# A planner's margin in front of TensorE steps goes from 80 to 200, and its table of ranks is replaced

## The chip, the cores and the metric

The kernel runs on one core of a Trainium2 chip. The metric is the device time of one execution in microseconds (us). Before the change the median of three runs is 565.36 us (565.08 to 565.58). The engines are TensorE (PE in the profile, PEld for its weight loads), VectorE (DVE), ScalarE (ACT), GpSimd (POOL) and SyncE (SP, which here only issues DMAs).

## The reference

Two layers over 2048 tokens of width 640 in bf16, each an attention block and a feed-forward block on layer-normed input, both with a residual:

```python
x = A_x
x = x + _A_ref(_layernorm(x), A_wq, A_wk, A_wv, A_wo, A_beta)
x = x + _B_ref(_layernorm(x), B_w1, B_w2)
x = x + _A_ref(_layernorm(x), A_wq, A_wk, A_wv, A_wo, A_beta)
x = x + _B_ref(_layernorm(x), B_w1, B_w2)
```

`_B_ref` is relu(x w1) w2 with an inner width of 1728. `_A_ref` has 32 heads of width 20 and goes through four segments of 512 tokens one after the other. Within a segment it is causal softmax attention; beside it each head reads a memory matrix M (20 x 20) and a vector z that were summed over the earlier segments, and the two results are mixed by a gate per head:

```python
logits = einsum('bhqd,bhkd->bhqk', qs, ks) * scale + mask
p = softmax(logits); a_dot = einsum('bhqk,bhkd->bhqd', p, vs)
a_mem = (phi(qs) @ M) / (phi(qs) @ z + 1e-6)
o = g * a_mem + (1 - g) * a_dot
M = M + phi(ks)^T vs;  z = z + sum(phi(ks))
```

## The kernel before

**The work.** There are eight segment passes: layer 0, segments 0 to 3, and layer 1, segments 0 to 3. A pass consists of `ln1` (layer norm and its transposition), `proj_kq` (L951, the keys and queries), `proj_v` (L998), `relay` (the last twelve rows of each head group are moved to a second tile, `kqL`), `scores` (L1290), `apply` (L1372), `mem_write` (L1153), `mem_read` (L1240), `o_turn`, `out_proj` (L1536), `ln2` and `ffn` (L1590 for w1, L1602 for its rest, L1620 for w2). One pass has 20 rounds of scores, so 160 in all. A round needs two PSUM slots of two banks each, X and Y, both free: TensorE fills them with a few narrow matmuls, ScalarE takes the exponential of each (L1304 and, where two head groups share a round, L1301), GpSimd masks the diagonal blocks (L1280), and the next round can start. Three more PSUM banks, MISC, serve all other matmul groups; VectorE or ScalarE empties them.

**What sets the order.** Nothing in the engines' streams is ordered by hand. Each of the parts above is a Python generator, and the class `Sched` simulates all engines with fixed costs and picks one step after another. The order in which it picks them is the order of the instructions on each engine; on the chip each instruction then waits for its semaphores and for nothing else. So a number of the planner changes the chip's time only through the order. (And through filler: where TensorE's planned gap, less 150, leaves room for two or more 128-wide matmuls, `_filled` emits that many matmuls on the identity, L779.) For each candidate step `_best` computes the earliest start, L292:

```python
r = ready + SEM_NS + (PE_MARGIN if e == "pe" else 0.0)
```

`ready` is the planned end of the last of the results and slots that the step needs. The candidate with the earliest start wins; between steps of the same start, the one with the lower `due`. The costs are in `mm_ns`, `dve_ns`, `act_ns` and `xbar`; a change of TensorE's mode (full array, `row` for scores, `col` for apply, `half` for L1602) is planned at `MODE_NS` = 100. The planner also holds packed VectorE operations and GpSimd's operations apart (`port`), and the crossbar transposes have the constants `XB_NS`, `XB_TILE`, `XB_LAT` at L163.

**The dues.** `plan` is run twice. The first plan takes its dues from the paced streams (`paced`, `each`) and serves only to list the keys of all steps. The second takes `due` from `TABLE`: a packed list of differences, one for each step of the sorted keys, whose running sum is the rank of that step (`ranked`). There are 5082 steps, and the ranks are a permutation of 0 to 5081. So the table says which of several steps that could start at the same time goes first; it doesn't fix the order by itself.

**The loads.** SP and ACT fetch the first four token tiles, wv, wk and wq; POOL fetches the other tokens, wo, w1 and w2 later, each DMA waiting for the one before (`loads_pool`). w2 lies over the keys and values of the first pass and is fetched after that pass is done with them.

Of the kernel before, what the change touches and what calls it, by code (L numbers as in the profile page):

```python
# [13 lines left out]
T = 2048  # L14
D = 640
H = 32
DH = 20
NSEG = 4
L = T // NSEG
# [3 lines left out]
G = H // 4  # L23
# [134 lines left out]


SEM_NS = 60.0  # L160
PE_MARGIN = 80.0

XB_NS, XB_TILE, XB_LAT = 200.0, 27.0, 2300.0  # L163
MODE_NS = 100.0
# [25 lines left out]
class Sched:  # L190
# [89 lines left out]
    def _best(self, op, resv=None):  # L280
# [10 lines left out]
        for k, (e, hold, tail, make) in enumerate(op.alts):  # L291
            r = ready + SEM_NS + (PE_MARGIN if e == "pe" else 0.0)  # L292
            if e == "dve" and op.port:
# [118 lines left out]


TABLE = """
c-
n1R3$UbBaqjcK=AZZ6xpVK_yZ5p8?t595eYq@;1$JR!c?v{8kw79EETSf2qA4q(QWdQz<Y6UPL9HYtWYIEZV#TCVR5YmslLBKBtPm=ZQV~UwW!
b&UF6`cC=j-pB`DZR=P0i!~&pF+Fy8Cp0-T!QJd!-~dOIb4cp<XB>@?J?Lk+12nRPfp^Z^36-
UeV1`#rGSypWwAwuExCEu&N@lJfj!m>MChq&ZIo4TS4<CjBJ+U`m|nv8F$Jzbr<H$;q$a!Cv|B_j@29Sz67hLr6b?g2jri0w=8Q-
y0WNiG4>X$ZDBl?{h+x?YBCBc-`6qlIRpw05-;e449SI<)xc{}_d(8W5`jkp?<vgMi8~I|w&43byd&)6a?pD_=%w<a-
YW;>eC%pW{!^!LZx`m;tZ{HGLkBr%tIlI58P@wf@5WeL4uk$MMxV!?a`~b@g8Q%N>yRji>_(*|-  # L420
_aZJYa4#GF*66%A*{>6C&G9IGG2_|b<mvGtD%Qo_*KR1??UHJcF;Bs``U)PdnwC`e)Pm1?0>&p3)}6IJ#q#3z7y|jWvd*N3t*XD@(%3jR?N9w*
2x{<u@|zx8+*J5JNgjxcNlZu4SqMtFUsAxelK=(6=r=zHsJT2Shqp01OMyg98fwecj4FhptT?RJomLjkm?`d4J-
O#@GU_PpIba6PwS#ONc%^yV$R)NApfR&u+xavO0hTCES|uQGii!>nb~auBP~!F0-Xui@?p6K-
eVSN<CS5ojNb{ZKMD<g3u{wIa#&{Nlx~DnZS15C9!*fGgK7@X*o^n}@>y`mWG!|wfwk-KYYo2bl?U!s_}h9=eFA)HSib>&If>cl;{Gu1bwG6ss
LwzXyCB{Bu%d!>LzufBJhsYN?Sfhhv`yxVAc1+sTGB7!eN?w&b_aWJ;ob)B$ziXf@+$O{z`M4Bb4+hYq0<sprSzXBR*!)87&yHIeVaeV;O*oaJ
XtAb=J>YvR?N=jIo$$n*WfXm<PY^{aWBGq0-
qVR?_~X43!ia#C!Argm}lGJmkW0y`e<)%k3z)XahTVmYIkD!W4(_f{g;haIHR}LQ?GzmG{DVfrSO{!+K8~L1$t5$r=r49lWq~3Q8oRnsOc$|`!
O;aXg-4Lt4K?+W?5Cu!foo^d~Z6)>7_C*_FXRcyYShYWplEyM?b?X6^D5yOG3I);2HBXDQGpqu6x&c&{Pucoz-
%<7tvy8)a$}zPYe6l{2J({ytZ#IOLdh@#&uYZ@Ol|CoP)V5n(#WOm)N(BlsIBkY~?VmR)#F&xMO>ofd_T)t4wYs+<i@_@p}lXUWQG~PmjUh%`O
S7^gUhD1+^%Z1!=vNGg*T6-p~d(wm`pvxjp$!_X+)cNqas};eJdfQDKLzh@J_gTc$7kSSLZ%RxRsE9i_ZEuN_Z<l75AL5e-  # L430
<;_L+l|r(^Sa8tYrm>$gS!^EU9SM=&oVl^iF~@qCx%4<re8bcIi+)J%`_DQ&K@V5QKC_mCX2N8!B1!N1*4IVJPRhP^R=Z@WCJy%{c0&%!zF-
;bonB__w7kN0)!cd()^=pbTrj<|C0oJ0l9SjvUZxgc{c5fMWi&cEMHGT`}Hpq~|IBO)C?K8Ep9Sf@Hf8ed|@H$SO{`F3}S7BY=B3jJvCp8o!tg
`T2;y~e?UCV?_?BwSr8ex;1NZa{Wd_)tPVt%9m6?A3dh26R6-?gr+&fid?}#`>?A5g-
c@B_iJN6vwEE>VU5dA!FE_^##`w<9WjPGaGE?<QH%!#oT`MPKr3~BSv4oI`tHT&b&se_8P6yKvbLnhZxZc(R3bKtiLIu#;f$vw^_U@{zn6vU(K
m+MSGPBy9{dEBaCQO{&F}ijy|}g=0T+pzk6$H!DmxwHUctjQh%>$CFsG?w*I8X#U3L>vYc@wLd>osE=`3o$830!{CCJ=r!kt4hw3upltrr)>&+
TV;PVpXX@_{&+hr5fESj1R*cmX5zN(IK&D$=O*F#+JuQ{!T$Q47PO4#$VdXFw+2MMT@Lqy3aX&L-
2&m`eI$E0s7Kd*Oi{UXoCB4{r$V)~UaaLbR>#}uRKb-
m0TGzZRHFX!3!&H9y9v8Oh0x?B;3E3(L4dfIVe|DMg<svI4?=}sg*f~AGW`t@lMnG$+u6mo^n9xjYUj4yrKClQPMUCS_S=)Z><T#+*zqeuUq*Z
PWP%rk~UmzXclhPY>T8j%-t9ak@CDRA=|j=9p?U^zr3&+%)>u#F($Qa}b3*f|SX%V*k@+-3`HCBY_++1_i!<SK>J?xUx_TM2l|5qa3!Qt-
)T)LO^j+b3}~gIcMJ`bPDA@{qm)uQxg`0%tDj_jSFzUmjCK1Ygyo`g8J>-YI{AN=Ws;^dTV8am@NPxnJk>S^YhE0=%BXno-nFcgx51wEn654)p  # L440
9$jXc1!G_OAZDn8AeKc~+C<(Gqg%|8}_Tuy7x1I`AFIOxSOHE|9;pVu>*2mSTVX~ffaT7Aw_jf%{4R{iNXixc*GutOE=hOje_kUnzkI%ci&SQA
g<H0(hoWfemmuM%R3;r}-3vK!?mh$%DB(<~yjMVGhXuGMfgyjyr>j6FGC4ZNpfL;J(Hw-xg<R4YFtpL88mEL&KoSaoPs(#x)i&ni|9qgENF9N%
-7U_}Fz%iuQzYIS*jZk+M5MGTvSeMYO|jbk)3zvznh>2iSr1~Xa`GEtd1cqN>cQqa4N-b5sj(~s-H23GZ&MbZIO;sVmJc#?z@*o)gqxT-
LcdKpUL<YfbSBf*|`NK(Z9nE2DOcn`Uq2~pgmlRj>b0yekU)F}{7{Y|+eCGCILi+H`L`->QPexR5H{F8=V`Bm)!DqcI0^rM-tHWKD=7siqTcU9
sV>A3+U=vW0NMXi>HeC08$=Q35qIWM7~TMbcUN#hXXmvshynBmM>RJzBllQdxEtU&J>z0_9@GeK{0K<14%<>#N^Oqa;F#EwhPyZUiGE9~<)xb@
|agO$^OC@mwVq+~I<#5@qO7WTAi)ZGd!I#kqAQP8d{>d8Ki_>9|06crOMd+(~P!d$)%@fu#ztk{|P>j~{+WYa{o$O`jnCv`#lo^Kj{Y|f&Vga6
+y*UNj5|98u;%H3FJU6?E78o2_pd}1+|<9a!CavC(hO}&~7Ejg-
=vB_iU8hkUB@2aouO)Fh|e_bO+7xVG|!TV9IvWL=wm8_5QTWY<g68P)`x3YXpV|E~F>{w;IZc^XZ$Q_t>J$UUwgqy?;ty5z$wG&RR>C!ZQ5cmH
AQEd-&vRl0uR+-
T&j55oRp~}eBmA#PR@8Txr)@A!jj(Bwh(JPZ{xu2>$sYmn?%4eOiR4$FIpEV=LR?HF?GM?J~CUJH`>$Wj_2FUils3x00_eU$^lwpXS!;~GtRK|  # L450
&XwqWj7yw^u-*e5)`QbA;{GlotuI=rTvC1<y!0V)UZedMI-SxMbp(RI<T=x^M?`I5X<OYGS==<P6O{wDM`&f0VbyKld(W+Cen9T4k<K14g!Fyo
+1L@n?hlEctto0*_a6qYmg+BrWY&%lm*vCEsII{P&n)v9|tg)QvCDwI0>t4_a*aZ(Rq)y}8^FB+C}S)(16e^JxC_sdkOtS&cz+X2kq99884(Av
-Q<fQj$*0;{8X>AhoE&$ixkE|a$CY$t_?w~h$+vc=DgVr+L?Zn!nu!D8k?xnno0i*S5CVx&1>)wdb=YfA??m2}vy7Enp>6;nG_RAMEWkk0w=*#
-JTA!<f>sfi%tDjGH$DfKGjJ_NlaHH<+b0+l@#L8EY+djN6k_YLbb$W^AkTSGnC*@YguL@&JD^z@jpRaV5OU^ReWZ;|9+kc>+#_9ZPZ7`O1#Ln
MF#()no7L4%zFe~UG+T-cSu?t|`>l28jR;5`d?{}#IZ|4g8cH5XEu5s3dEb+{)5TQ-
7=lBWiswTfdAFndc)#zc5Qjc}Ug*IjPXa0+*FlO2NTrb~ZH1E<zlXJ`3aMpR5W$)q^%&E(zq3?7X`;&&r*MYuawOc@Ml4rOMpU#-
^NANw4S5tPfub2@fKTa)LCK!f)T#T!K)f>RGi`PE(+-t-iWxP!GF>oHn7$Q%!9U5!O<;cHwPOXc34(RS<*EM1XKMVb+Q8`~eDc3<aHQ27k4ps-
WW-z{oQqE$YsKx#D?qQ6XpWMe-K1J)ACT7^hZ$pv;pftiWXU`s{SuMYH?$cN`#QyP6h}jWOO&1#bAY-DTz8ujz3OTlh_XF_!wbWc5D(HyyvsGq
y(K^$Ng0I5^;?Uul*Si>BtP5S1R=}W5)?XGcCZRcdn$ZMh-
?y`Kx!+yMPI*R+?vxJEM$E|ZF`TCotJGG=f*zB#<yYjxw95)`a3+<2dM!qu0mmC5T^ZV}QI=XjDmhN^ZO~j595%AE?CS!H`6q#4FM}?-  # L460
JR|Rb7x~WcY3z6Qv~|J8*}I+x9zOx}`3CBO9Y6r*VdOQ}V)nfd9Bqe(To>_Z7}}e~^@#kfi`ZX32NG|FTpw^}^aa!p9|WgKNbwZrw;{_GBHFqv
VNQb@9D+V_`NCWe>C_999|aV#5^C~Z_thhxG$5F0pabXYKSM)LI_u0gafZ_Zw=HQ@pvg4ggpH{B##o=_MJ<>PbPp_w7(#df2;HzxuUFT@L6gu=
Z}u^G<|g)}Ew`+J{)Sk2WdYfgLs!FAA9A)LFQl%q$6X0N)8sts{?}xIUD`H%Bw-
!rv6`L0@qp1)A9HW+E=KSISM*);kZr~oZ)|ioeaR79_ABI`6>f3ys_srybXuc;-
~HX;FrE%n^EuIH6guTGW9&n2K}VsJobhL{S01nGrX57gjs|M<IN<31?z|M@;!yYYDu@MW`-
uL0$X53LOMNHT_7Py29pdefcAmI7DL8!&{@20v9L6mIO++R5Wm~@Ls&X$p`qvTX4<V!eue02Hz5JD{AgZmAkGr~j241|*jqzE}?Z;K8LG`Fscp
8tPu3rQC$JKY7U*+=(+q*rpxQ56s2gM^RXVk6gfczQWmqL=Yp}U$f|HZ(YksL=>wdnpf-mQuu&MKt5#bp8i<jhfLUCO9qr`0+YUuIviArHDNWd
0#o5b-~%Fj{w6!CoRib{T7kj1?w4d2UJ!Yo&YwXJ~Z-8oUry@j6zvP0Y#gYZ;N_GF1EfC~KARe-
<;x5Ft{mIjbFfE@D=f^1iOyKyOhk!k^MEJMZfef7f7^Jz=#~Q;>U1#wlH0UPLU|4ysqk57{;7Ad8&B%r3pIgn3(W?xw^#5!<2tG3H~~2lRH3(j
?>=2OnR@b%+(Z>`~8R&bUkyr>w=^c4Phq>}ee+Zv>Y$SUG~ZqZl3H{#uZzLrU9Vaf|zHXm>%+WhS3MoL<l8-  # L470
&3Hv0R9d3Ypok#v2PtUGs`~5PVk=Q6PYQZvT68n7b{2Tm4^{m%gp0lR(C7<9z^r)(C09pI5%;B98xVpzT=43Cv`1%UE;_xb~OtA)8uFLruc+o6
7LB_c(cb0pZFiwE;Z9)-
fs}~8iM)d6KQyoo%4BRLLY0h)~hk*#zdiI;`WTSMv2)yXWUY?NN?1ZwNB6M)$w)6WP7kKs(IQs)UbtR;1*9wg_yO*C*~zcWO292Y?%fWn38*qa
`c{pm04d^nI$q_Wqb;p^B)N@XVjS!az>Awb!bkcRw9*zTodsXTf%Nm9I#)R)kSabS$G~{{TTZnMVr*Cz_h#ZIl++%ck8RUD(0CVRYSMF%<nc)Z
jI5vSBH7vU*}ayjF|)!krNM%u=-DVWn*=sxoX%;ovVHAUg4A2JnW^!)fHl%l=VoN+R12Z-vb&Z+H7!kllVBJ?uMzCGx{!h3Yn)t4VzD-
)I$O<9^=kDl1alq8yb+cLaWz<<-DC*jA*qWX+jNm7^!ov%h(IBZdi=-
XY+>{x8guKV*RzOhVv|ko?=B*BaSH(|M^Ip@nqVJ4mFU`nk7E5s<3xvHfmApmEc8&WRC$uMXV*-
)P!|TeZAMFw|MQl;Q34N;Tm_jmpdu5KCA>ktTWztX>$HHtDGCKX&Nx4{g>oc*{5HD$3Msa2zV}L_i<9}NuRUAirG1h=~dpgWoo6u-
bhOQ=E3h1UT4e!Ilancw5Jt4&&h+A4D%`5I-
Y|@IN2@C?9dBiV9%#C3LaDqepHiQA2mb#>5}6p{NXgD+jAnJcK=yFirMc+q%kVvI2~2)>jR+Mkr(u8M4yA;enZs8%C(?p(Q!q;<Wff5wX7UU@+  # L480
`8jWv5?41~fkZ;nsl4QN0nfHiF`#ZZptn9XqfS*p&NE{zK@`=izymS<*j&|GHcjo|f3NjwUj6hx7g(IPMw!Z1I#S4qZIoIeSqbE>Kgy8{NlCd8
iod-%BoZ8hf~83wG)Tkmwk4%`l`r5dMo%VyAKma-7jxfyfrv-
}c>rh}A+Ix`rwLL*&Af(L6kliRI#`IUrR|^jP9QED~C5j`(!&Nu|eD{^XuwZ?yvi?O09B$V>VuS03nGYO(KR;OR(QV84uBw!%1JShG9ulsh4=U
C{^K6@^Y+(Ftx0;Juz~_i&$8<h;Yg)JgGd((_#oNdG1Izwm#6l+ngNuWN-4brk-
eWRY`>_;k2H#71Sh*h!!NpUZb(u^oK!wW&bDlSQ{XD{Q-_&_q%^N%ED6|G!f4ADojtpYiqC8hE?yDdy9PNd6y@&HNb
"""


def one(fn):
    return lambda *s: [(lambda e: fn(e, *s), True)]  # L490


def pe(ns, make, waits=(), acq=(), users=1, mode="full", hold=()):
    return Op([("pe", ns, 190.0, make)], waits, acq, users, mode, hold=hold)

# [1219 lines left out]
```

## Time and profile before

| | |
|---|---|
| median of three runs | 565.36 us |
| the profiled execution | 565.58 us, span 563.8 us (1.8 us outside the span) |
| TensorE matmul | 5115 instructions, 556.4 us busy (99%) |
| VectorE, ScalarE, GpSimd | 420.9, 422.5, 214.9 us busy |
| granted TensorE clock | 1.000 over the span |
| first matmul; first scores; first w1 matmul; last scores | 1.25; 19.07; 108.73; 472.96 us |

A busy matmul time of 99% says little by itself: each matmul is shown with its whole way through the array, so neighbours overlap. What a matmul costs is the distance from its start to the next one's start. Where the page says that an engine was idle before an instruction, it names what ended the idle time.

### The profile page before, as it was taken

What the parts mean: (1) busy time and instruction counts of PE and PEld (TensorE: products, weight loads), DVE (VectorE), ACT (ScalarE), POOL (GpSimd) and SP (SyncE); (2) the same over time, 40 slices, a digit from 0 to 9 for tenths busy, and PEclk for the clock granted to TensorE, in tenths of its full rate; (3) what the DMA queues carried; (4) which work ended last, traced back from release to release, by engine and by line L of the source; (5) the groups of instructions that cost most, each with busy time, mean ns of one, the idle gap of its engine ahead of it and who ended that gap; (6) DMA issues with size and microseconds to landing.
All of it is one profiled execution on the core that took longest, in us unless ns stands there. A gap on an engine that the chain in (4) does not pass through costs nothing.

```text
span 563.8 us, 12521 instructions
## 1 busy us (share of the span) xinstructions
PE 556.4 (99%) x5115; PEld 297.7 (53%) x5118; DVE 420.9 (75%) x1024; ACT 422.5 (75%) x517; POOL 214.9 (38%) x341
## 2 busy tenths in 40 slices
PE   8999999999999999999999999999999999999997
PEld 5454455445555445644546454565545654755655
DVE  6789989998998878857689956998778876424202
ACT  3899999999889878688897978878898778023140
POOL 3664546454454343452345433244333443002000
PEclk9999999999999999999999999999999999999999
DMA  6435787776534343573255451565116531431201
GB/s 221 129 90 133 152 145 150 226 153 106 90 70 85 57 72 62 81 119 76 44 82 106 80 84 20 96 124 93 33 19 91 99 82 20 86 73 36 59 1 47
DMA packets 126609, 50.62 MB, mean 90 GB/s; under 512 B 112120, under 2 KB 124600, under 8 KB 126552
## 3 DMA queue, kind: packets, MB, share of 16 engines
q1 hardware_dynamic: 124568, 42.19, 40.3%
q0 software_dynamic: 1552, 7.29, 4.5%
q8 instruction: 40, 0.66, 0.5%
q10 hardware_dynamic: 432, 0.34, 0.2%
q14 instruction: 17, 0.14, 0.1%
HBM read 15.16 MB, written 7.37 MB: 40 GB/s over the span
## 4 chain that ended last, share of the span: by engine, by line
PE 91%; DVE 5%; ACT 2%; DMA 1%; issue 0%; SPq 0%
PE ps L1590 21%; PE ps L1620 20%; PE ps L951 15%; PE ps L1290 9%; PE ps L998 8%; PE ps L1536 7%; PE ps L1372 7%; DMA wv_r<-in_A_wv_dram 1%; PE ps L1153 1%; PE ps L1240 1%; ACT PT L1304 1%; DVE x_sb L1478 1%; PE ps L1602 1%; DVE stats L868 1%; DVE stats L869 1%; PE ps L1096 1%
## 5 line engine op out<-in xcount | busy, mean ns | idle before, releaser
L1304 ACT ACTIVATE PT<-ps 128x1024 bf16<-128x1024 f32 x256 | 248.3, 1024 | 42.9 <-PE ps L1290 42.1
L1280 POOL TENSOR_SCALAR_AFFINE_SELECT PT<-PT 128x512 bf16<-128x512 bf16 x256 | 173.1, 692 | 235.8 <-ACT PT L1304 195.5
L1620 PE MATMUL ps<-wb,hT 128*128 128x320 bf16 x896 | 133.0, 300 | 0.1
L1590 PE MATMUL ps<-xnT,wb 128*128 128x512 bf16 x520 | 127.4, 380 | 0.0
L1478 DVE TENSOR_TENSOR x_sb<-x_sb,ps 128x320 bf16<-128x320 bf16 x128 | 60.7, 479 | 73.3 <-PE ps L1620 49.5
L1620 PEld LDWEIGHTS ps<-wb,hT 128*128 128x128 bf16 x896 | 84.2, 98 | 37.5 <-issue 5.9
L1572 ACT ACTIVATE hT<-ps 128x512 bf16<-128x512 f32 (+1 forms) x65 | 37.4, 577 | 54.5 <-PE ps L1590 53.9
L1590 PEld LDWEIGHTS ps<-xnT,wb 128*128 128x128 bf16 x520 | 47.2, 98 | 54.8 <-issue 7.6
L1301 ACT ACTIVATE PT<-ps 128x1024 bf16<-128x1024 f32 x64 | 62.1, 1024 | 12.2 <-PE ps L1290 12.0
L998 PE MATMUL ps<-wv_r,xnT 128*128 128x320 bf16 x320 | 57.0, 300 | 0.9 <-DMA wv_r<-in_A_wv_dram 0.8
L951 PE MATMUL ps<-xnT,wq_p 128*128 128x512 bf16 x200 | 55.8, 380 | 0.1
L951 PE MATMUL ps<-xnT,wk_p 128*128 128x512 bf16 x200 | 54.9, 380 | 0.0
L1536 PE MATMUL ps<-wo_r,oT 128*128 128x320 bf16 x280 | 50.2, 300 | 0.0
L1571 DVE TENSOR_SCALAR hT<-ps 128x512 bf16<-128x512 f32 (+1 forms) x47 | 31.9, 680 | 12.9 <-PE ps L1590 12.6
L1372 PE MATMUL ps<-PT,va 128*32 128x128 bf16 (+3 forms) x896 | 40.8, 302 | 0.0
L998 PEld LDWEIGHTS ps<-wv_r,xnT 128*128 128x128 bf16 x320 | 29.6, 98 | 20.8 <-issue 2.6
L938 DVE CAST kq<-ps 128x512 bf16<-128x512 f32 x43 | 29.4, 683 | 10.0 <-PE ps L951 9.6
L1290 PE MATMUL ps<-kq 20*128 20x512 bf16 (+3 forms) x560 | 35.3, 301 | 1.2 <-ACT PT L1304 1.2
L1536 PEld LDWEIGHTS ps<-wo_r,oT 128*128 128x128 bf16 x280 | 26.8, 98 | 15.5 <-issue 2.0
L881 DVE TENSOR_SCALAR xn_tok<-x_sb,mv,rstd 128x640 bf16<-128x640 bf16 x64 | 30.0, 482 | 3.2 <-POOL rstd L877 3.1
L868 DVE BATCH_NORM_STATS2 stats<-x_sb 128x6 f32<-128x320 bf16 x64 | 30.1, 471 | 1.6 <-DMA x_sb<-in_A_x_dram 1.4
L1372 PEld LDWEIGHTS ps<-PT,va 128*32 128x32 bf16 x896 | 18.9, 96 | 21.9 <-issue 11.0
(112 smaller groups left out, 620.7 us busy)
## 6 DMA issues: line engine op xcount, KB each, us to landing
kq_scr<-kq SPq DMA_DIRECT2D x28, 120.0 KB
kqL<-kq_scr SPq DMA_DIRECT2D x28, 120.0 KB
out_dram<-x_sb SPq DMA_DIRECT2D x16, 160.0 KB, 2.0
wb<-in_B_w_dram POOLq DMA_DIRECT2D x5, 432.0 KB, 4.2
x_sb<-in_A_x_dram POOLq DMA_DIRECT2D x3, 640.0 KB, 5.3
wb<-in_B_w_dram POOLq DMA_DIRECT2D x2, 640.0 KB, 5.8
kq_away<-hT SPq DMA_DIRECT2D x5, 256.0 KB, 4.8
kq<-kq_away SPq DMA_DIRECT2D x5, 256.0 KB, 5.1
```

Of the source, the lines that this page charges most:

```text
L951: fn = lambda e, bank, k=k, w_p=w_p, c=c: e.matmul(bank, w_p[:, k, c * 128:(c + 1) * 128], xnT[:, k_, :, k, :], start=(k == 0), stop=(k == ...
L998: fn = lambda e, bank, k=k, i=i, hf=hf: e.matmul(bank[:, 0:320], xnT[:, k_, i, k, :], wv_r[:, k, hf * 320:(hf + 1) * 320], start=(k == 0), ...
L1280: tm = yield pool(590.0, lambda e: e.affine_select(out=reg, in_=reg, pattern=[[0, 4], [1, 128]], compare_op=ALU.is_ge, fill=0.0, base=0, c ...
L1290: fns.append((lambda e, x=x, j=j, hh=hh, N=N, o=o: e.matmul(ps[:, hh, o:o + N], kq(b, gg[x], 0)[32 * hh:32 * hh + DH, 128 * j:128 * j + 12 ...
L1301: fn = lambda e: e.activation(PT[:, :, 2 * k:2 * k + 2, 1024:1280], bs.ap.rearrange("p h (x t) -> p x h t", x=2), ACT.Exp, scale=SCALE)
L1304: fn = lambda e: e.activation(PT[:, items[0], 2 * k:2 * k + 2, c0:c0 + 512], bs.ap, ACT.Exp, scale=SCALE)
L1372: return [(lambda e, hh=hh, j=j: e.matmul(bank[32 * hh:32 * hh + 32, 128 * j:L], v_flat[b][:, (j * H + 8 * hh + g) * E1:(j * H + 8 * hh + ...
L1478: ta = yield dve(320, 1, lambda e: e.tensor_tensor(xa, xa, bk.ap[:, 0:320], ALU.add), [tk], early=HOT)
L1536: fn = lambda e, bank, k=k, hf=hf, o=ot.ap: e.matmul(bank[:, 0:320], o[:, k, :], wo_r[:, k, hf * 320:(hf + 1) * 320], start=(k == 0), stop ...
L1572: lambda e: e.activation(d, bk.ap[:, 0:n], ACT.Relu), [tk] + hs[0].old + (hs[1].old if dc >= NSTG // L else []))
L1590: fn = lambda e, bank, k=k, dc=dc: e.matmul(bank, w1_r[:, k, dc * 128:(dc + 1) * 128], xnT[:, k_, :, k, :], start=(k == 0), stop=(k == FC ...
L1620: fn = lambda e, bank, dc=dc, q=q, h=h, hf=hf: e.matmul(bank[:, 0:320], h, w2_r[:, q, hf * 320:(hf + 1) * 320], start=(dc == 0), stop=(dc ...
```

## The change

`PE_MARGIN` goes from 80 to 200, and `TABLE` is another one. These are all the lines that differ. The port rule of the planner and the crossbar constants are the same in both kernels.

```diff
 SEM_NS = 60.0
-PE_MARGIN = 80.0
+PE_MARGIN = 200.0
 
 XB_NS, XB_TILE, XB_LAT = 200.0, 27.0, 2300.0
...
 TABLE = """
-c-
-n1R3$UbBaqjcK=AZZ6xpVK_yZ5p8?t595eYq@;1$JR!c?v{8kw79EETSf2qA4q(QWdQz<Y6UPL9HYtWYIEZV#TCVR5YmslLBKBtPm=ZQV~UwW!
...
+c-mcBX^>o3bv|!@y-
+iO~&vehC8ELdHmaG+7vLs_!c5J*Tw#o)C!P!XJ;D8O7m{jtED*hxzxkzwq0)(nmB{&HoA&@F6j;T<DB2EDn949P^aj;ClHd;ouq}k`>JKw$Ubx
...
 """
```

Read as `ranked` reads them, both tables hold a permutation of 0 to 5081 for the same 5082 steps. 144 steps keep their rank, the median step moves by 13 places, the farthest by 292. If TensorE's 2832 steps stood in the order of their ranks, its mode would change 414 times by the old table and 410 times by the new one; the last scores step would be number 2296 by the old and number 2309 by the new, the last apply step number 2316 and 2323. The twelve steps of the loads of w1 and w2 on POOL move to lower ranks with one exception (15 higher), by 1 to 179 places, the last of them from 1155 to 1122.

## The prediction

> **What bounds the kernel now.** I read the page first, then TensorE's waits, then stretches of the span, then the timeline of a few transitions. The page's totals and clock, and TensorE's waits:
>
> ```profile
> PE 556.4 (99%) x5115; PEld 297.7 (53%) x5118; DVE 420.9 (75%) x1024; ACT 422.5 (75%) x517; POOL 214.9 (38%) x341
> ...
> PEclk9999999999999999999999999999999999999999
> ...
> L1304 ACT ACTIVATE PT<-ps 128x1024 bf16<-128x1024 f32 x256 | 248.3, 1024 | 42.9 <-PE ps L1290 42.1
> ```
>
> ```profile
> PE ps L820 <- DVE ktok L817: 1.2, 1, 1.2
> PE ps L1290 <- ACT PT L1304: 1.2, 2, 0.8
> PE ps L998 <- DMA wv_r<-in_A_wv_dram: 0.8, 1, 0.8
> PE ps L1240 <- DVE o_sb L1229: 0.4, 1, 0.4
> PE ps L845 <- ACT xnT L853: 0.2, 1, 0.2
> PE ps L1096 <- issue: 0.2, 1, 0.2
> ```
>
> The reader is to see that TensorE bounds the kernel and idles 4.0 us in all. Of these 1.2 and 0.8 us lie in the start (warm-up, first weights). What remains that a margin could cover is a wait on ScalarE or VectorE: 1.2 + 0.4 + 0.2 = 1.8 us.
>
> Busy time isn't cost, so the chain has to confirm this. Its pieces in order of time end with
>
> ```profile
> 531.00 14.03 PE ps L1590 x65
> 545.69 15.33 PE ps L1620 x112
> ```
>
> 65 matmuls of 512 columns in 14.03 us are 216 ns each, 112 of 320 columns in 15.33 us are 137 ns each. These are the starts' distances in the long runs, and the groups' means of 380 and 300 ns are latencies. The Trainium skill, "Perfetto Trace Analysis", section "Identifying the Most-Contended Engine", holds matmul busy time for a bad measure and takes the share of weight loads in its place. That share is 53% here, which read alone would leave TensorE room and promise a gain of many tens of us; the 216 and 137 ns rows say that nothing is left in the long runs, and the sum below goes by them.
>
> Next, stretches: from the first scores to the first w1 matmul, then to 200, to 480, and to the end (columns: length; busy time and instructions of PE, PEld, DVE, ACT, POOL; clock; DMA):
>
> ```profile
> 17.00:108.70 91.70, 90.78 (x878) 44.83 (x879) 82.16 (x204) 87.26 (x110) 52.55 (x87) 1.00 0.64 139
> 108.70:200.00 91.30, 89.92 (x906) 47.01 (x904) 82.04 (x200) 83.06 (x97) 41.18 (x59) 1.00 0.55 104
> 200.00:480.00 280.00, 279.89 (x2704) 147.06 (x2705) 221.56 (x523) 227.63 (x267) 111.62 (x168) 1.00 0.42 74
> 480.00:563.80 83.80, 81.01 (x538) 50.21 (x526) 23.57 (x56) 16.89 (x29) 3.82 (x9) 1.00 0.22 51
> ```
>
> The stage that matters is the first: ScalarE is busy 95% of it, VectorE 90% and TensorE 99%, and no feed-forward matmul exists yet that could fill a hole. From 200 us on the other two have room, and in the last stretch TensorE works alone on its store of feed-forward work.
>
> **The change part by part.** No instruction's work changes; 5082 steps are the same, only their order on each engine (and the filler) may differ. So each term is a difference of waiting.
>
> *Waits that the margin removes.* A step that reads another engine's result is planned 120 ns later, so that work on hand goes in front of it. At most the 1.8 us above go, at least nothing, since each of these four waits may return elsewhere. I take half: -0.9 us.
>
> *Scores rounds that come later.* The nearest row for how close they run now is that of the weight loads' waits:
>
> ```profile
> PEld ps L1290 <- ACT PT L1304: 22.2, 61, 0.9
> ...
> PEld ps L1290 <- ACT PT L1301: 5.8, 17, 0.4
> ```
>
> In 78 cases of some 160 rounds the weight load stood ready for the exponential, while the matmuls before it still ran; only in two did TensorE really idle. The planned order is thus already tight, and 120 ns more puts another matmul ahead of the round: one of 216 ns in 56% of the rounds, or one of 137 ns in 88%, either way 0.12 us a round on average. ScalarE, which waits 42.9 us for scores in the L1304 row, would wait up to 160 x 0.12 = 19 us longer in all. Behind its late exponentials stand in its queue the PSUM evictions for TensorE's next groups, the masks on POOL, and through them apply. Where feed-forward work is on hand, TensorE doesn't notice: the last scores are at 472.96 us, and 80 us of TensorE's own work follow, so 19 us fit. Before 108.70 nothing is on hand but projections, which run ahead only as far as three buffers for keys and values let them. Of the 1024 scores matmuls 216 lie in 17 to 108.7 us, so 34 rounds: up to 34 x 0.12 = 4.1 us, nearly all of ScalarE's idle 91.70 - 87.26 = 4.4 us there. The lower end is 0, or what the table brings earlier; by ranks the last scores step moves from number 2296 to 2309 among TensorE's 2832 steps, hence nothing speaks for earlier. I take half of 4.1: +2.0 us.
>
> *New waits of a new order.* 4938 of 5082 ranks differ. Short stalls can come anywhere: a long VectorE or ScalarE operation in front of the eviction that TensorE needs. No row of before prices them; the nearest is the list of waits without the first two starts' items, 2.0 us for the whole of the present order. A new one may have none of them (that gain is counted already) or several times as many. I take half of this sum more: +1.0, ends 0 and +6 (three times as many).
>
> *Mode changes.* What one costs is seen on TensorE's timeline:
>
> ```profile
> 413.73 0.38 PE L951 MATMUL ps<-xnT,wq_p 128*128 128x512 bf16 x1
> 414.05 0.39 PE L1290 MATMUL ps<-kqL 20*128 20x512 bf16 x4
> 414.37 1.04 PE L951 MATMUL ps<-xnT,wq_p 128*128 128x512 bf16 x4
> ```
>
> The scores start 320 ns after a matmul that costs 216, so a change costs 0.10 us. The trace of before has 399 changes between the lines of scores, apply, L1602 and the rest. In rank order the tables give 414 and 410, so -0.4 us if the planner treats them alike; a later apply could also part from the round it now follows directly (43 times), some 10 changes each way: ends -1.4 and +1.0, taken 0.
>
> *Filler.* 26 filler matmuls lie at 6 to 8 us, while TensorE waits for the first tokens and for wv, and cost nothing under that cover. A margin of 120 more makes room for two more at 56 ns where a gap is planned. Without cover ten such places would cost 10 x 2 x 56 = 1.1 us; taken 0, its end kept in the range.
>
> *Queues.* The loads on POOL move to lower ranks by up to 179 places. The last w2 piece is issued at 121.97 and the first L1620 is at 130.89, while such a load lands in about 4.2 us by the page; 4.7 us are in hand. On SP the transposes keep their number. Both 0, as long as POOL isn't delayed by 4.7 us.
>
> Sum: -0.9 + 2.0 + 1.0 + 0 = +2.1 us. The profiled run was at 565.58 us, 0.22 above the median; 565.58 + 2.1 = 567.7, and against the median 567.5. I say 567.6.
>
> **The rivals.**
>
> *Slightly slower (the forecast)*: 566.5 to 570.5, the terms between a quarter and twice their value.
>
> *The margin pays (the other side)*: scores in the first stretch aren't later, because there a projection matmul was ahead of them anyhow, and the 1.8 us go, with a few mode changes: 565.4 - 1.8 - 0.4 = 563.2. For it: the wait at 159.56 us, where four scores matmuls idle 0.78 us with w2 matmuls on hand that could have gone first, just what a margin is for. Against it: two such cases in 160 rounds. It decides when the first stretch loses less than 0.9 us.
>
> *Nothing moves beyond measurement*: TensorE's 541.6 us of work in 17 to 563.8 us hide all of it, 565.4.
>
> *Starved for longer*: the first stretch loses its full 4.1 us, and the second, where ScalarE is busy 91% and VectorE 90%, the same way, 204 of 1024 scores matmuls or 32 rounds, 3.8 us: 565.4 - 0.9 + 7.9 + 1.0 = 573.4. Against it: from 108.73 on feed-forward work is on hand. In these holes the clock is a risk of its own: the warm-up, 14 matmuls of 512 columns in 5.12 us, shows 0.43 us between starts in place of 0.216. By the Trainium skill, "TensorE: Matmul & The Clock Gate", section "HAM oscillation", idling beyond about 3.4 us brings the slow clock back; one such hole would add an estimated 1.7 us by that page. No run here shows it, and the longest idle here is 1.2 us at clock 1.000; I add nothing.
>
> **How the numbers follow.** 0.2% of 565.36 is 1.1 us, about what a measurement can tell from no change. Slightly slower 0.42, starved 0.14, nothing 0.16, the margin pays 0.28. So faster 0.28, same 0.16, slower 0.56. The range takes in the other side down to 563.2 less the mode changes' further 1.0 us, and the starved case up to 573.4 plus the filler's 1.1: 562.2 to 574.5. The forecast's own range is 566.5 to 570.5.
>
> **What would show it.** The first w1 matmul later than 108.73 by about 2 us, and more ScalarE idle before L1304 than 42.9 us (50 to 62) with fewer than 78 waits of weight loads. TensorE idle of over 3 us in 17 to 108.7 us in place of 0.9. Mode changes within 389 to 409. I would be wrong if scores kept their pace in the first stretch, if the filler reached the middle of the kernel, or if a single long wait, say on a transpose or on w2, outweighed all of these.

## The result: 567.66 us, slower by 0.4%

The changed kernel takes 567.66 us (median of four, 567.54 to 567.81), the kernel before 565.47 us beside it; the ratio is 1.0040 with an interval of 1.0023 to 1.0058. The profiled execution took 567.76 us, its span is 566.0 us. All four ran at a granted clock of 1.000; some executions of one and the same kernel further down show less and last longer (the kernel before in one set of runs: a median of 565.29 us at 1.000 and of 567.23 us at 0.997), so the comparisons below go by the executions at 1.000 where there are any. `TABLE` is two lines longer, so every line below it has a number higher by two: L1292 is the scores' line, L1306 and L1303 the exponentials', L1592 and L1622 the two feed-forward lines, L953 keys and queries.

The page's totals and the groups of exponentials and masks, after:

```profile
PE 557.1 (98%) x5112; PEld 297.0 (52%) x5115; DVE 419.1 (74%) x1018; ACT 426.5 (75%) x523; POOL 208.9 (37%) x341
...
L1306 ACT ACTIVATE PT<-ps 128x1024 bf16<-128x1024 f32 x256 | 248.2, 1022 | 44.0 <-PE ps L1292 43.2
L1282 POOL TENSOR_SCALAR_AFFINE_SELECT PT<-PT 128x512 bf16<-128x512 bf16 x256 | 167.8, 671 | 255.3 <-ACT PT L1306 211.4
```

TensorE's waits, after:

```profile
PE ps L1292 <- ACT PT L1306: 1.9, 4, 1.1
PE ps L822 <- DVE ktok L819: 1.2, 1, 1.2
PE ps L1155 <- DVE x_sb L1480: 0.7, 1, 0.7
PE ps L847 <- DVE xn_tok L883: 0.6, 2, 0.3
PE ps L953 <- DVE o_sb L1457: 0.4, 1, 0.4
PE ps L1292 <- ACT PT L1303: 0.3, 1, 0.3
PE ps L1242 <- DVE x_sb L1480: 0.2, 1, 0.2
PE ps L1374 <- POOL PT L1282: 0.2, 1, 0.2
```

The waits on a result of ScalarE, VectorE or GpSimd, warm-up left out, add up to 4.3 us where before had 1.8. The busy columns of the same stretches as in the prediction (length; PE, PEld, DVE, ACT, POOL; clock, DMA):

```profile
17.00:108.70 91.70, 89.84 (x865) 44.06 (x867) 80.20 (x200) 87.10 (x111) 50.94 (x84) 1.00 0.64 140
108.70:200.00 91.30, 88.93 (x900) 45.47 (x899) 82.46 (x198) 81.83 (x97) 40.03 (x60) 1.00 0.53 97
200.00:480.00 280.00, 280.00 (x2693) 147.49 (x2692) 217.51 (x514) 230.92 (x270) 106.15 (x165) 1.00 0.47 75
480.00:566.00 86.00, 83.19 (x558) 51.30 (x555) 27.64 (x68) 18.46 (x32) 5.54 (x12) 1.00 0.23 50
```

TensorE idles 91.70 - 89.84 = 1.86 us in the first stretch (before: 0.92) and 2.37 us in the second (before: 1.38). That is 1.9 us of the 2.2 us. From 200 to 480 us TensorE has next to no idle in either kernel (0.11 us before, 0.00 after), and the last two runs of matmuls have the same length as before:

```profile
533.18 14.03 PE ps L1592 x65
...
547.87 15.34 PE ps L1622 x112
```

TensorE changes its mode 399 times in both kernels, and the filler is 23 matmuls, all ahead of 8.1 us, in place of 26. So the loss isn't spread over the kernel. It sits in a handful of places, the largest within five microseconds (TensorE's timeline, after):

```profile
170.48 0.81 PE L1155 MATMUL ps<-va,ktok 128*128 128x84 bf16 x16 [0.71 <-DVE x_sb L1480]
171.13 0.71 PE L1622 MATMUL ps<-wb,hT 128*128 128x320 bf16 x4
171.77 0.40 PE L1292 MATMUL ps<-kqL 20*128 20x512 bf16 x4
172.34 0.73 PE L1374 MATMUL ps<-PT,va 128*32 128x512 bf16 x16 [0.17 <-POOL PT L1282]
174.19 0.40 PE L1292 MATMUL ps<-kqL 20*128 20x384 bf16 x8 [1.12 <-ACT PT L1306]
174.52 0.82 PE L1592 MATMUL ps<-xnT,wb 128*128 128x512 bf16 x3
```

Here the first feed-forward block has just ended and the second is about to begin. TensorE waits for a PSUM bank that VectorE empties (0.71), for a mask, and then for exponentials (1.12), with nothing to put between apply and the next scores. Only at 174.52 do the next w1 matmuls start. That is 2.0 us of idle in one place. Before has its own such place at 159.56 to 160.37 us, worth 0.78 + 0.41 us (its timeline):

```profile
159.56 0.29 PE L1290 MATMUL ps<-kq 20*128 20x256 bf16 x4 [0.78 <-ACT PT L1304]
...
160.37 0.33 PE L1240 MATMUL ps<-BD,phq 128*128 128x84 bf16 x4 [0.41 <-DVE o_sb L1229]
...
160.76 0.79 PEld L1620 LDWEIGHTS ps<-wb,hT 128*128 128x128 bf16 x7 [0.21 <-DVE o_sb L1229]
```

### The profile page after: what moved, and what is told of

Same layout as the page of the kernel before. It is cut to its first block, busy times and chain, and to the rows that moved or that the text cites. A ratio compares the mean times of both kernels' runs of the same rounds, so it can differ in the third digit from the quotient of the medians.

```text
span 566.0 us, 12510 instructions
## 1 busy us (share of the span) xinstructions
PE 557.1 (98%) x5112; PEld 297.0 (52%) x5115; DVE 419.1 (74%) x1018; ACT 426.5 (75%) x523; POOL 208.9 (37%) x341
## 4 chain that ended last, share of the span: by engine, by line
PE 88%; DVE 7%; ACT 4%; DMA 1%; issue 0%; DVEq 0%
PE ps L1622 20%; PE ps L1592 20%; PE ps L953 14%; PE ps L1292 8%; PE ps L1000 8%; PE ps L1538 7%; PE ps L1374 7%; ACT PT L1306 3%; PE ps L1155 1%; PE ps L1242 1%; DVE x_sb L1480 1%; PE ps L1604 1%; DVE ktok L1148 1%; DVE stats L870 1%; DVE stats L871 1%; DVE xn_tok L883 1%
## 5 line engine op out<-in xcount | busy, mean ns | idle before, releaser
L1306 ACT ACTIVATE PT<-ps 128x1024 bf16<-128x1024 f32 x256 | 248.2, 1022 | 44.0 <-PE ps L1292 43.2
L1282 POOL TENSOR_SCALAR_AFFINE_SELECT PT<-PT 128x512 bf16<-128x512 bf16 x256 | 167.8, 671 | 255.3 <-ACT PT L1306 211.4
L1622 PE MATMUL ps<-wb,hT 128*128 128x320 bf16 x896 | 136.0, 300 | 0.0
L1592 PE MATMUL ps<-xnT,wb 128*128 128x512 bf16 x520 | 127.0, 380 | 0.0
L1622 PEld LDWEIGHTS ps<-wb,hT 128*128 128x128 bf16 x896 | 83.8, 98 | 37.8 <-issue 6.5
L1592 PEld LDWEIGHTS ps<-xnT,wb 128*128 128x128 bf16 x520 | 47.6, 98 | 54.9 <-issue 6.9
L1574 ACT ACTIVATE hT<-ps 128x512 bf16<-128x512 f32 (+1 forms) x60 | 34.4, 575 | 51.9 <-PE ps L1592 51.2
L1303 ACT ACTIVATE PT<-ps 128x1024 bf16<-128x1024 f32 x64 | 62.5, 1030 | 10.4 <-PE ps L1292 10.3
L953 PE MATMUL ps<-xnT,wk_p 128*128 128x512 bf16 x200 | 55.5, 380 | 0.4 <-DVE o_sb L1457 0.4
L953 PE MATMUL ps<-xnT,wq_p 128*128 128x512 bf16 x200 | 55.1, 380 | 0.1
L1573 DVE TENSOR_SCALAR hT<-ps 128x512 bf16<-128x512 f32 (+1 forms) x52 | 35.1, 680 | 11.3 <-PE ps L1592 10.5
L1292 PE MATMUL ps<-kq 20*128 20x512 bf16 (+3 forms) x560 | 35.3, 301 | 0.8 <-ACT PT L1306 0.8
L940 DVE CAST kq<-ps 128x512 bf16<-128x512 f32 x40 | 27.3, 686 | 11.6 <-PE ps L953 11.3
```

Of the source, the lines that this page charges most:

```text
L953: fn = lambda e, bank, k=k, w_p=w_p, c=c: e.matmul(bank, w_p[:, k, c * 128:(c + 1) * 128], xnT[:, k_, :, k, :], start=(k == 0), stop=(k == ...
L1282: tm = yield pool(590.0, lambda e: e.affine_select(out=reg, in_=reg, pattern=[[0, 4], [1, 128]], compare_op=ALU.is_ge, fill=0.0, base=0, c ...
L1292: fns.append((lambda e, x=x, j=j, hh=hh, N=N, o=o: e.matmul(ps[:, hh, o:o + N], kq(b, gg[x], 0)[32 * hh:32 * hh + DH, 128 * j:128 * j + 12 ...
L1303: fn = lambda e: e.activation(PT[:, :, 2 * k:2 * k + 2, 1024:1280], bs.ap.rearrange("p h (x t) -> p x h t", x=2), ACT.Exp, scale=SCALE)
L1306: fn = lambda e: e.activation(PT[:, items[0], 2 * k:2 * k + 2, c0:c0 + 512], bs.ap, ACT.Exp, scale=SCALE)
L1592: fn = lambda e, bank, k=k, dc=dc: e.matmul(bank, w1_r[:, k, dc * 128:(dc + 1) * 128], xnT[:, k_, :, k, :], start=(k == 0), stop=(k == FC ...
```

## The experiments

All times are medians, of all executions and of those at a granted clock of 1.000 alone (in brackets how many these are). Idle is TensorE's, the stretch's length less the busy time, in 17 to 108.7, 108.7 to 200 and 200 to 480 us of the profiled execution; the clock of that execution was 0.994 for the old table with margin 200, 0.997 for the new table with margin 80 and for rounds later, and 1.000 for all others. The ratio is to the kernel before, run on the same chip, over all executions.

| kernel | us | ratio (interval) | us at clock 1.000 | idle, us |
|---|---|---|---|---|
| before | 565.4 | 1 | 565.3 (51 of 70) | 0.92, 1.38, 0.11 |
| after | 567.66 | 1.0040 (1.0023 to 1.0058) | 567.66 (4 of 4) | 1.86, 2.37, 0.00 |
| old table, margin 200 | 581.48 | 1.0278 (1.0253 to 1.0304) | none of 4 | 3.00, 5.20, 2.53 |
| new table, margin 80 | 579.11 | 1.0233 (1.0213 to 1.0252) | 578.35 (2 of 4) | 3.70, 2.87, 2.19 |
| light additions, before | 565.16 | 0.9991 (0.9979 to 1.0003) | 565.09 (9 of 10) | 0.92, 1.42, 0.11 |
| light additions, after | 567.04 | 1.0022 (1.0012 to 1.0033) | 567.04 (8 of 8) | 1.86, 1.95, 0.00 |
| short exponentials, before | 568.99 | 1.0061 (1.0047 to 1.0076) | 568.41 (3 of 6) | 1.25, 3.07, 0.11 |
| short exponentials, after | 569.19 | 1.0065 (1.0051 to 1.0079) | 568.47 (2 of 6) | 1.53, 2.74, 0.00 |
| small masks, before | 564.90 | 0.9999 (0.9986 to 1.0011) | 564.81 (8 of 12) | 0.66, 1.26, 0.11 |
| small masks, after | 566.26 | 1.0012 (1.0004 to 1.0021) | 566.26 (9 of 11) | 1.36, 1.70, 0.00 |
| rounds later, before | 569.67 | 1.0071 (1.0054 to 1.0088) | 569.50 (4 of 6) | 2.03, 2.52, 0.11 |
| rounds earlier, after | 570.56 | 1.0086 (1.0071 to 1.0100) | 570.56 (6 of 6) | 1.71, 3.03, 0.00 |
| rounds earlier, before | 567.51 | 1.0032 (1.0019 to 1.0045) | 567.49 (7 of 8) | 0.86, 1.82, 0.11 |
| rounds earlier, after, apply kept | 571.61 | 1.0113 (1.0096 to 1.0130) | 571.61 (4 of 4) | 2.73, 3.47, 0.00 |

**1 and 2. One part of the change alone.** The margin with the old table, and the new table with the margin of before:

```diff
-PE_MARGIN = 80.0
+PE_MARGIN = 200.0     # the table of before stays
```

> The margin alone: 200 with the table of before. Theory A (margin and table belong together; a margin that the ranks weren't made for holds scores rounds back where TensorE has no feed-forward work yet): slower than both kernels, 570 to 578 us, by the prediction's 4.1 us in the first stretch and 3.8 us in the second, with TensorE idle of 5 us or more between 17 and 200 us (before: 2.3 us). Rival B (the margin alone carries the 2.2 us, the ranks are neutral): 567.0 to 568.5 us. Rival C (the table alone carries it): 565 to 566 us.

```diff
-PE_MARGIN = 200.0     # in the changed kernel
+PE_MARGIN = 80.0
```

> The table alone: the new ranks with margin 80. Theory A (the two belong together): slower than the kernel before, 567 to 575 us, since these ranks weren't made for this margin. Rival B (the margin carries the 2.2 us): 565 to 566 us. Rival C (the table carries it): 567.0 to 568.5 us.

Measured: 581.48 and 579.11 us. Neither part carries the 2.2 us: each alone costs 13 to 16 us, and both together cost 2.2. Rivals B and C fall. That margin and table belong together, as theory A says, holds, but both values lie above its ranges. The clock line of the margin alone and its stretches:

```profile
PEclk9999999999989999999999899999999999999999
...
17.00:108.70 91.70, 88.70 (x848) 43.08 (x849) 78.52 (x194) 84.45 (x108) 50.44 (x83) 1.00 0.66 133
108.70:200.00 91.30, 86.10 (x878) 44.94 (x874) 78.51 (x187) 79.56 (x94) 39.51 (x57) 0.98 0.54 104
200.00:480.00 280.00, 277.47 (x2655) 145.27 (x2648) 209.70 (x502) 231.82 (x276) 106.80 (x163) 0.99 0.45 74
```

All three engines fall back in the same stretches: against before, in 17 to 200 us, TensorE has 5.9 us less work done, VectorE 7.2 and ScalarE 6.3. The idle goes up by 8.3 us in 17 to 480 us. Three things that theory A doesn't have come on top. The granted clock was 0.50 from 167.2 to 170.6 us and from 327.6 to 331.0 us (the two 8s of the clock line), where TensorE counts as busy all the same: twelve matmuls of L1620 from 166.88 us on take 3.10 us, 258 ns each in place of 137. By half of 2 x 3.4 us that is an estimated 3.4 us. There are 47 fillers in place of 26, the last at 181 us, so up to 21 x 56 ns = 1.2 us, and 406 changes of mode in place of 399, 0.7 us. Some 2.6 us of the 16.2 us in span stay unplaced. The new table with margin 80 has one such fall of the clock (from 325.0 us, an estimated 1.7 us), 56 fillers (the last at 249.8 us, up to 1.7 us), 420 changes of mode (2.1 us) and 6.4 us more idle, 11.9 of its 13.9 us together. Here a table of ranks is worth its time only at the margin for which it stands.

**3 and 4. Is a late VectorE the cause?** Sixteen residual additions take 32 of 320 columns, in each kernel with its own order:

```diff
-xa = x_sb[:, t, 320 * hf:320 * hf + 320]
+w = 32 if key[0:3] in (("xA", 0, 1), ("xB", 0, 0)) else 320
+xa = x_sb[:, t, 320 * hf:320 * hf + w]
```

> Leaves out nine tenths of sixteen residual additions (those of the first feed-forward block's tiles of segment 0 and of the first output projection's of segment 1), with the order and the planned costs kept: each takes 32 of 320 columns, so VectorE has some 4 us less work between about 113 and 170 us. If TensorE's waits in 108.7 to 200 us come from a late VectorE, the waits at 160.4 us (0.4 us) shrink: 0.3 to 0.8 us faster than before. If they come from the place of scores in the order and ScalarE's exponentials, no change: within 0.2 us.

> The same sixteen additions cut in the changed kernel, order and planned costs kept. If a late VectorE makes the waits around 170 to 175 us (0.7 and 1.1 us of idle there), 1.0 to 2.0 us faster than the changed kernel, so 565.7 to 566.7 us, and the idle at 170.48 us is gone. If the order of scores and ScalarE's exponentials make them, at most 0.3 us faster: 567.4 us or more.

Measured: 565.16 and 567.04 us. After gains 0.6 us, less than the 1.0 to 2.0 expected of a late VectorE and more than the 0.3 of its rival. Before gains 0.3 us at clock 1.000 (565.09 against 565.37), the lower end of what a late VectorE was to give; over all executions its interval reaches over 1. In after the wait of 0.71 us at 170.48 is gone from the list, but the wait of apply for a mask, 0.2 us, has become 0.7 us:

```profile
PE ps L1374 <- POOL PT L1282: 0.7, 1, 0.7
```

A wait took the place of the one removed. The distance between the two kernels only goes from 2.2 to 1.9 us, so these additions carry some 0.3 us of the change: a small part, not the cause.

**5 and 6. Are late exponentials the cause?** Half of the columns of 88 exponentials before 200 us:

```diff
-fn = lambda e: e.activation(PT[:, items[0], 2*k:2*k+2, c0:c0 + 512], bs.ap, ACT.Exp, scale=SCALE)
+w = 256 if 1 <= m < 12 else 512
+fn = lambda e: e.activation(PT[:, items[0], 2*k:2*k+2, c0:c0 + w], bs.ap[:, :, 0:w], ACT.Exp, scale=SCALE)
```

> Leaves out half of the columns of the one-head-group exponentials (L1304's kind) of eleven of the first twelve pairs of head groups, so that ScalarE has some 0.4 us less to do in 88 of its instructions before about 200 us; order and planned costs are kept. The first stretch has 0.9 us of TensorE idle and 108.7 to 200 us has 1.4 us. If ScalarE's lateness there makes the waits, nearly all of the 2.3 us go: 563.0 to 564.2 us. If VectorE, the transposes or the order make them, 564.8 to 565.5 us.

> The same in the changed kernel, whose idle in the two stretches is 1.9 and 2.4 us. If the changed kernel's 2.2 us are waits behind late exponentials before 200 us (the prediction's term of scores rounds that come later), they go and the two kernels with short exponentials lie within 0.6 us of each other: 563.2 to 564.6 us. If the 2.2 us come from elsewhere (VectorE, transposes, mode changes), the distance between the two stays 1.5 us or more: 566.0 us or more.

Measured: 568.99 and 569.19 us, at clock 1.000 568.41 and 568.47. The two kernels come within 0.2 us, as the theory asked, but on the wrong side: with 34 us less work on ScalarE both are slower, by 3.1 and 0.8 us at clock 1.000. No expectation had that. The waits of scores for exponentials did shrink, from 1.2 to 0.2 us in before and from 2.2 to 0.5 us in after, but others came in their place, so the runs neither show late exponentials to be the cause nor rule them out. In before the new waits are for VectorE:

```profile
PE ps L1240 <- DVE phq L1210: 1.2, 1, 1.2
PE ps L1240 <- DVE o_sb L1229: 1.2, 1, 1.2
PE ps L845 <- DVE xn_tok L881: 0.6, 1, 0.6
PE ps L1153 <- DVE ktok L1146: 0.6, 1, 0.6
```

In after the longest is for a transposition by DMA:

```profile
PE ps L1593 <- DMA xnT<-xn_tok: 1.4, 1, 1.4
```

The first of the waits in before is seen in the timeline. In before, with long exponentials, the same VectorE instructions:

```profile
172.15 0.50 DVE L1173 TENSOR_TENSOR BD<-M_sb,maskg 128x336 bf16<-128x336 f32 x1
172.57 0.20 DVE L870 BATCH_NORM_AGGREGATE mv<-stats 128x2 f32<-128x12 f32 x1
172.69 0.64 DVE L1210 TENSOR_TENSOR phq<-phq,etmp 128x1024 bf16<-128x1024 bf16 x1
```

and with short exponentials:

```profile
174.11 1.69 POOL L1280 TENSOR_SCALAR_AFFINE_SELECT PT<-PT 128x512 bf16<-128x512 bf16 x2 [2.21 <-ACT PT L1305]
174.37 0.93 DVE L1173 TENSOR_TENSOR BD<-M_sb,maskg 128x336 bf16<-128x336 f32 x1
...
175.35 1.00 DVE L1210 TENSOR_TENSOR phq<-phq,etmp 128x1024 bf16<-128x1024 bf16 x1
...
176.40 0.33 PE L1240 MATMUL ps<-BD,phq 128*128 128x84 bf16 x4 [1.21 <-DVE phq L1210]
```

With the exponentials shorter the masks come at another moment of VectorE's work, beside L1173 and L1210. The two took 0.93 and 1.00 us in place of 0.50 and 0.64, and two masks took 1.69 us where a mask alone takes 0.63. The Trainium skill, "SBUF — State Buffer", section "Who interferes with whom", says that a VectorE instruction with two inputs in SBUF contends with a GpSimd instruction that reads SBUF, for a port pair that only one of them holds at a time. The rows agree in kind: the two VectorE instructions take some 0.4 us longer each, and the two masks some 0.4 us longer together. L1173 is such an instruction and is not a packed one: the planner's `port` is set where `mode > 1` and doesn't know of it.

**7 and 8. What do these meetings cost?** The masks of the first twelve pairs take 16 columns of each 128, in each kernel with its own order:

```diff
-reg = PT[:, x, :, PT_OFF[j]:PT_OFF[j] + 128]
+w = 16 if m < 12 else 128
+reg = PT[:, x, :, PT_OFF[j]:PT_OFF[j] + w]     # and pattern=[[0, 4], [1, w]]
```

> Leaves out seven eighths of the causal masks of the first twelve pairs of head groups (16 of 128 columns in each block), so GpSimd's masks before about 200 us become short; order and planned costs are kept. Measured against the short ones of the same shape, VectorE's instructions in 17 to 200 us are stretched by 8.3 us in the kernel before and 10.2 us in the changed one, and the masks by 8.5 and 5.9 us. If what holds TensorE up there is VectorE and GpSimd stretching each other, most of that goes and TensorE's idle of 2.3 us in 17 to 200 us goes below 1.2 us: 563.5 to 564.7 us. If the stretching doesn't matter to TensorE, within 0.4 us of before.

> The same in the changed kernel (idle 4.2 us in 17 to 200 us). If VectorE's stretching by GpSimd makes the difference between the two kernels, they come within 0.7 us of each other, and this one is at 563.8 to 565.3 us. If the order of TensorE's steps makes it, the distance stays 1.5 us or more.

Measured: 564.90 and 566.26 us. By how much VectorE's instructions are stretched I count as what each takes over the shortest tenth of its own line and shape, in eight of these kernels, where that is over 40 ns. In 17 to 200 us it is 8.1 us in before and 9.9 us in after; with small masks it is 3.1 and 2.8 us. At clock 1.000 the two kernels take 564.81 and 566.26 us, so their distance goes from 2.2 to 1.4 us. So the long masks make up about 0.8 us of the change's 2.2 us, by meeting VectorE's work or because apply has to wait for them; the run doesn't part the two. 1.4 us stay, and neither kernel did as expected: after misses its range by 1.0 us on the slow side, and before gains 0.5 us, with 1.92 us of idle in 17 to 200 us where less than 1.2 was named.

**9 to 12. Does the place of scores rounds decide?** To move rounds and nothing else, the finished order of a kernel is replayed step by step on all engines, with chosen scores steps one place later or earlier among TensorE's steps; the orders of VectorE, ScalarE, GpSimd and SP are untouched, and filler is kept to the first 20 us:

```diff
-P, S = plan(ranked(S))
+dues = ranked(S)
+P, S = plan(dues)
+P, S = plan(dues, moved(S, MOVES))   # MOVES = {1: 1, 2: 1, ...} rounds and places
```

> The order of the kernel before, word for word on every engine, with 46 of the scores rounds 1 to 65 (those in 21 to 198 us that are not followed by apply) placed behind the one matmul that now follows them. That holds each back by 137 or 216 ns, some 8 us in all; the changed kernel holds its rounds of 17 to 200 us back by 5.4 us in all against before. If rounds that come later cost TensorE's time there (the prediction's term), 2 to 4 us slower: 567.4 to 569.5 us. If only chance meetings of VectorE and GpSimd do, within 1 us of before.

> The order of the changed kernel, with 38 of the scores rounds 1 to 65 (those that start so long after their exponentials that a matmul fits in) placed ahead of the one matmul that now precedes them: some 6.8 us earlier in all. If later rounds are what made the changed kernel slower, the 2.2 us go for the most part: 565.0 to 566.4 us. If not, 567.2 us or more.

> The same move in the kernel before, 30 rounds, some 5.3 us earlier in all. If earlier rounds pay in general, 563.8 to 565.0 us. If the present places are what VectorE and GpSimd need, no gain: 565.2 us or more.

> The changed kernel's order with 25 of its scores rounds 1 to 65 placed ahead of the one matmul that precedes them, only such rounds as no apply follows, so that TensorE keeps its 399 changes of mode (the run before it had 412, 1.3 us more by 0.10 us each): some 4.3 us earlier in all. If the later rounds made the changed kernel slower and the mode changes spoilt the run before, 565.6 to 566.9 us. If every displacement costs, whichever way it goes, 567.6 us or more.

Measured, as the lag of a scores round behind the end of the exponential before it (read from the rows of L1290, L1304 and L1301; lags over 1.5 us, where a round waits for something else, left out of the sums):

| kernel | lag in 17 to 108.7 us, sum | 108.7 to 200, sum | 200 to 480, median of a round | us |
|---|---|---|---|---|
| before | 8.9 | 10.0 | 0.345 | 565.4 |
| after | 10.2 | 14.1 | 0.491 | 567.66 |
| rounds later, before | 12.0 | 12.4 | 0.347 | 569.67 |
| rounds earlier, after | 9.3 | 13.4 | 0.504 | 570.56 |
| rounds earlier, before | 7.9 | 11.1 | 0.345 | 567.51 |
| rounds earlier, after, apply kept | 9.3 | 14.0 | 0.504 | 571.61 |

The change does hold rounds back: 5.4 us in 17 to 200 us and 0.146 us a round after that, where nothing is lost. And holding the rounds of before back by as much (3.1 + 2.4 = 5.5 us) costs 4.2 us, the upper end of the range that was named and about twice what the change costs. Its largest wait is one on VectorE again:

```profile
163.56 0.46 PE L1274 MATMUL ps<-BD,phq 128*128 128x84 bf16 x4 [1.58 <-DVE o_sb L1263]
```

But the other direction pays nothing back. Earlier rounds make after slower by 2.9 us and before by 2.1 us. More changes of mode explain 1.3 us of the first (412 in place of 399; a matmul came to stand between a round and the apply behind it) and 0.9 us of the second (408), but with apply kept and 399 changes after is at 571.61. The lags are hardly shorter (by 1.6 us in after where some 6.8 were planned, by 1.0 us with apply kept where 4.3 were): what a round gains by its place it loses to something before it, so what rounds would cost that really start earlier isn't shown. Later rounds are enough to cost what the change costs, and are not shown to be its cause; each of the four displacements costs, whichever way it goes.

No run beat the kernel before by more than its uncertainty without leaving work out.

## Why the prediction was right or wrong

*The bound and the headroom* held. TensorE had 4.0 us of idle to give, nothing was won, and the whole move is 2.2 us. The first two stretches are where it happens, and from 200 us on TensorE's store of feed-forward work takes the new order without idle, as was said. It doesn't take any order: with one part of the change alone 2.5 and 2.2 us of idle appear in 200 to 480 us.

*Waits that the margin removes, -0.9*: wrong in sign. The waits on other engines' results went from 1.8 to 4.3 us, those of scores on exponentials from 1.2 to 2.2 us. The near waits of the weight loads did become fewer (78 before, 44 + 10 after), which the prediction's last part had asked for, but they cost nothing before. One argument in the rival was wrong as well: at 159.56 us no w2 matmul stood ready to go first. The next one, at 160.76, begins a new group, and its weight load waited 0.21 us for the bank that L1229 had to empty.

*Scores rounds that come later, +2.0*: the delay was right in size where TensorE has work on hand, 0.146 us a round after 200 us against 0.12 predicted, and 4.1 us in 108.7 to 200 us where the starved rival had 3.8; in the first stretch it was 1.3 us where up to 4.1 were named. Its cost was placed wrongly. The step that failed is that from 108.70 us on feed-forward work is on hand and the delay costs nothing there: the first stretch lost 0.94 us of TensorE's time where 2.0 were taken (1.86 us of idle, not over 3), and 108.7 to 200 us another 0.99 us. The first block's feed-forward work runs out at 171.5 us, and the next starts at 174.52. How much of this ScalarE carries stays open. Its idle before L1304 went from 42.9 to 44.0 us where 50 to 62 were named, and less work on ScalarE made both kernels slower. Of the 4.3 us that TensorE waits in the changed kernel, 2.2 are for exponentials, 1.9 for banks and results that VectorE has to deliver, and 0.2 for a mask. The first w1 matmul moved from 108.73 to 109.72 us, half of the 2 us named.

*New waits of a new order, +1.0*: right in kind. This is where the loss is seen, in a few places of 0.2 to 1.1 us, against a gain of none.

*Mode changes and filler, 0*: right, 399 against 399, and 23 fillers at the start.

*The sum*, +2.1 against +2.2, is nearer than its terms: -0.9 was not there, +2.0 was 0.94 in the stretch for which it stood, and the second stretch's 0.99 was taken as nothing. The number came out since errors of opposite sign met, which is luck.

*The clock, 0*: right for the change, where it stayed at 1.000. But the fall that the prediction saw in no run came in the experiments, and without an idle of 3.4 us: when rounds were held back it came at the end of an idle of 1.58 us, and in the two runs with one part of the change no idle in the ten microseconds ahead of it is over 1.5 us. Which idle brings it on, no run tells.

*What stays open.* So the cause of the 2.2 us is shown only in part. About 0.8 us go with the masks and 0.3 us with VectorE's additions, and the two may overlap. With shorter exponentials the distance is gone, but at a higher time of both. What the rest is due to isn't shown. All seven other orders that were run (the changed one, those with one part alone, the four with rounds moved) are slower than the order before, by 2.1 to 16 us, which would fit an order that suits this kernel so well that any departure costs; no run tests that. Whether a margin of 200 must cost anything, with ranks better fitted to it, no run tells: no third table was run. Neither was a planner tried that keeps two-input VectorE instructions apart from the masks as well.

## What to carry to other kernels

When an order comes from a planner, its constants and its table of priorities are one object: change one alone and measure it, and it will look far worse (13 to 16 us here) than the pair does (2.2 us). Where the bound engine has no store of independent work, look there first for what a new order costs, and look at the engine that empties its buffers as well as at the one with the longest instructions. A saving on a side engine is no gain by itself: 34 us less on ScalarE made this kernel 3.1 us slower at the full clock, and at the one place that was followed, two VectorE instructions had come to run beside masks. Read the granted clock before comparing small differences: one fall of 3.4 us is worth nearly as much as the whole change here.

## What the runs showed of the hardware that wasn't expected

VectorE's L1173, a float32 product of two SBUF operands in no packed mode, takes 0.445 to 0.937 us for the same shape in one execution of before, and 0.93 us in the row above beside a mask; a packed-only rule for what may run beside GpSimd misses it. Masks of one shape take 0.624 to 1.304 us in after.

The granted clock fell to half for 3.4 us in the middle of a kernel that keeps TensorE busy. In rounds later, before, the row of that stretch is (length; PE, PEld, DVE, ACT, POOL; clock, DMA)

```profile
163.50:166.90 3.40, 3.34 (x22) 1.77 (x23) 3.37 (x14) 2.57 (x4) 1.16 (x3) 0.50 0.67 125
```

The executions of that kernel at 0.997, this one among them, take 570.99 us (median of two), those at 1.000 569.50. The busy share doesn't show such a fall, since slower matmuls count as busy.
